# Reordering the start of a Fourier-mixing and ReGLU kernel: x first, weights later, the second batch's bounce sooner

## The chip, the cores and the metric

One core of one Trainium2 chip runs the whole kernel. The metric is the device time in microseconds (us) of one execution; a median over several runs is given. Runs more than 1.5% above a kernel's fastest would be left out. A "span" is the time from the first to the last instruction of the one execution that was profiled; it is some 2 us below the device time.

## The reference, cut to what matters

```python
def _attn_ref(x, filt_r, filt_i):              # x: 8 batches of 3008 x 256
    X = np.fft.rfft(x, axis=1)
    Y = X * (filt_r + 1j * filt_i)[None]
    return np.fft.irfft(Y, n=x.shape[1], axis=1)

def _moe_ref(x, w_gate, w_val, w_out):         # 24064 tokens, 256 -> 1536 -> 256
    return (np.maximum(x @ w_gate, 0) * (x @ w_val)) @ w_out
```

Everything is float32 at the interface; the kernel works in bf16 after the first matmul.

## The kernel before

The length 3008 is split into 94 x 32. For each batch, stage A (a 94-point transform, `psA`) writes to DRAM (`Abuf`) and is read back transposed (`at`): this is "the bounce". Stage B does the forward 32-point transform (`psX`), the product with the filters (`tt`, `uu`) and the inverse (`psD`), and writes to DRAM again (`Dbuf`), which is read as `dC`. Stage C (`psY`) gives the tokens, and then the FFN runs in 47 blocks of 512 tokens with 12 steps each. From the first block on, the next batch's A, B and C are slipped into the steps of the FFN ("forward 0 of batch 1 at step 16"). Batch 0 and part of batch 1 have no FFN to hide in: that is the prologue, which the change touches.

Two queues of transfers matter. The sync engine issues x, tables, `Abuf`, `at`, `Dbuf`, `dC`, strictly in program order, each waiting for its data. GpSimd issues filters and weights, which are cast from float32 to bf16 on the way. Both run on the same 16 DMA engines (the DMA views below give each queue's share of them).

```python
    load_x(0, nc.sync, ((0, 0, 2 * q), (0, 2 * q, 4 * q), (1, 0, 2 * q)))
    nc.sync.dma_start(F2, ...)                     # tables
    nc.sync.dma_start(tabs, ...)
    load_x(0, nc.sync, ((1, 2 * q, 4 * q),))
    ...
    hold_gpsimd(XF[0][:, 2 * q - 8:2 * q])         # GpSimd waits for the first half of tile 0
    load_filters()
    load_own_filters()
    warm(11)
    for i, f in enumerate(items_a(0)):             # 16 items of A, fillers between them
        f()
        if i >= 13: make_back_t(i - 13)
        else:       warm(1, 256)
        ...
    # bounce, copies of the filters to their places, more fillers
    hold_gpsimd(ats[0][0:32, NG - 1, 0:8])         # bounce is in
    load_vg(0, DFF // 2)                           # first half of the two input weights
    nc.sync.dma_start(gate, ats[0][0:32, NG - 1, 0:8])   # the sync queue waits too
    load_x(1, nc.sync, ...)
    first_b(amid)                                  # B of batch 0, with items of A of batch 1
    load_d(0, 0, 1)                                # first quarter of dC
    # a 1-row read of Dbuf makes GpSimd wait for D
    load_vg(DFF // 2, DFF)                         # second half
    load_o()                                       # output weights
    for f in early: f()                            # the rest of A of batch 1
    ... # [cut] in the steps of the FFN: load_d(0, 1..3) at 0, 9, 14;
        # load_at(1, 0..3) at 3; forwards of batch 1 at 16, 23, 26, 29, 35, 40
```

## Time and profile before

| | before |
|---|---|
| device time, median of the runs beside the changed kernel | 907.38 us |
| span of the profiled run | 905.5 us |
| TensorE busy, whole span | 97% |
| first matmul of A / last end of A | 7.46 / 23.77 us |
| first forward of B (bounce is in) / first product | 33.44 / 33.89 us |
| last inverse of B ends | 54.55 us |
| first `psY` of C | 62.83 us |
| forward 0 of batch 1 | 87.63 us, at step 16 |

A row of the timeline names what ran and when it started; these moments are simply the first or last row of a tile. The stretches, the chain and the waits themselves are shown in the prediction.

### The profile page before, as it was taken

What the parts mean: (1) busy time and instruction counts of PE and PEld (TensorE: products, weight loads), DVE (VectorE), ACT (ScalarE), POOL (GpSimd) and SP (SyncE); (2) the same over time, 40 slices, a digit from 0 to 9 for tenths busy, and PEclk for the clock granted to TensorE, in tenths of its full rate; (3) what the DMA queues carried; (4) which work ended last, traced back from release to release, by engine and by line L of the source; (5) the groups of instructions that cost most, each with busy time, mean ns of one, the idle gap of its engine ahead of it and who ended that gap; (6) DMA issues with size and microseconds to landing.
All of it is one profiled execution on the core that took longest, in us unless ns stands there. A gap on an engine that the chain in (4) does not pass through costs nothing.

```text
span 905.5 us, 19111 instructions
## 1 busy us (share of the span) xinstructions
PE 875.3 (97%) x7096; PEld 512.1 (57%) x7217; DVE 566.6 (63%) x872; ACT 498.6 (55%) x891; POOL 359.0 (40%) x351
## 2 busy tenths in 40 slices
PE   8797899999999999999999999999999999999997
PEld 3343565556555665566655566556655556666665
DVE  2635776567665776657766677657766577655553
ACT  4474556555555555555655565655565555555552
POOL 4342667117680386614763166811768000000000
PEclk9899999999999999999999999999999999999999
DMA  9979337623475344663364533754346512331111
GB/s 254 245 219 220 101 95 177 141 80 109 122 175 118 90 126 122 141 134 112 96 161 128 119 98 101 182 116 100 108 136 158 116 31 82 78 75 36 37 32 51
DMA packets 113662, 109.17 MB, mean 121 GB/s; under 512 B 20290, under 2 KB 98370, under 8 KB 112834
## 3 DMA queue, kind: packets, MB, share of 16 engines
q1 hardware_dynamic: 91078, 81.72, 35.3%
q0 software_dynamic: 22176, 26.01, 11.7%
q8 instruction: 57, 0.93, 0.5%
q10 hardware_dynamic: 316, 0.22, 0.1%
q14 instruction: 35, 0.29, 0.1%
HBM read 61.93 MB, written 49.81 MB: 123 GB/s over the span
## 4 chain that ended last, share of the span: by engine, by line
PE 86%; DVE 4%; DMA 4%; ACT 3%; issue 1%; SPq 1%; POOL 0%; DVEq 0%; POOLq 0%
PE psG L464 25%; PE psO L483 25%; PE psV L464 24%; DVE prod L469 4%; PE psA L276 3%; PE psF L322 3%; ACT vsb L467 3%; PE psD L393 2%; PE psX L363 2%; PE psY L448 1%; DMA XF<-in_x_dram 1%; DMA dC<-Dbuf 1%; DMA Abuf<-asb 1%; DMA out_dram<-osb 0%; DMA at<-Abuf 0%
## 5 line engine op out<-in xcount | busy, mean ns | idle before, releaser
L469 DVE SCALAR_TENSOR_TENSOR prod<-psG,vsb 128x512 bf16<-128x512 f32 x564 | 389.0, 690 | 271.3 <-ACT vsb L467 265.8
L467 ACT CAST vsb<-psV 128x512 bf16<-128x512 f32 x564 | 333.0, 590 | 266.8 <-PE psV L464 211.7
L483 PE MATMUL psO<-WoT,prod 128*128 128x256 bf16 x2256 | 336.6, 273 | 1.5
L464 PE MATMUL psG<-yT,WgT 128*128 128x512 bf16 x1099 | 329.1, 379 | 7.4 <-DMA WgT<-in_moe_w_gate_dram 2.5
L464 PE MATMUL psV<-yT,WvT 128*128 128x512 bf16 x1037 | 316.9, 380 | 0.7 <-ACT yT L453 0.4
L483 PEld LDWEIGHTS <-prod 128*128 128x128 bf16 x2256 | 220.7, 98 | 143.4
L464 PEld LDWEIGHTS <-WgT 128*128 128x128 bf16 x1128 | 109.9, 98 | 136.9 <-DMA WgT<-in_moe_w_gate_dram 3.0
L464 PEld LDWEIGHTS <-WvT 128*128 128x128 bf16 x1128 | 98.1, 98 | 41.8 <-issue 30.4
L258 POOL CAST scr<-yT 128x8 f32<-128x8 bf16 x24 | 4.6, 191 | 265.8 <-ACT yT L453 265.8
L379 DVE TENSOR_TENSOR tt<-psX,Ftr 128x512 bf16<-128x512 f32 x96 | 65.0, 682 | 12.9 <-PE psX L363 12.9
L400 ACT CAST dsb<-psD 128x512 bf16<-128x512 f32 x96 | 51.5, 589 | 28.5 <-PE psD L393 28.4
L308 POOL TENSOR_TENSOR fold<-XP 128x1024 f32<-128x1024 f32 x24 | 56.5, 2356 | 25.1 <-PE psF L322 24.9
L489 ACT COPY osb<-psO 128x512 f32<-128x512 f32 x92 | 54.5, 593 | 20.6 <-PE psO L483 20.3
L379 DVE TENSOR_TENSOR uu<-psX,Fti 128x512 bf16<-128x512 f32 x89 | 60.6, 681 | 0.0
L309 POOL TENSOR_TENSOR XP<-XP 128x1024 f32<-128x1024 f32 x24 | 56.4, 2350 | 1.9
L295 POOL DMA_DIRECT2D XP<-in_x_dram x96 | 56.4, 592 | 0.9 <-issue 0.5
L453 ACT CAST yT<-psY 128x512 bf16<-128x512 f32 x47 | 27.6, 586 | 26.2 <-PE psY L448 26.2
L329 DVE CAST asb<-psF 128x512 bf16<-128x512 f32 x48 | 30.9, 686 | 17.3 <-PE psF L322 12.9
L329 ACT CAST asb<-psF 128x512 bf16<-128x512 f32 x48 | 25.8, 589 | 27.3 <-PE psF L322 27.3
L448 PE MATMUL psY<-M,dC 96*128 96x94 bf16 (+18 forms) x604 | 37.7, 198 | 1.1 <-DMA dC<-Dbuf 1.1
L455 DVE CAST yT<-psY 128x512 bf16<-128x512 f32 x47 | 32.0, 681 | 9.8 <-PE psY L448 9.8
L448 PEld LDWEIGHTS <-dC 96*128 96x128 bf16 x604 | 34.5, 97 | 4.6 <-DMA dC<-Dbuf 1.2
(66 smaller groups left out, 481.6 us busy)
## 6 DMA issues: line engine op xcount, KB each, us to landing
at<-Abuf SPq DMA_DIRECT2D x32, 384.0 KB
dC<-Dbuf SPq DMA_DIRECT2D x64, 192.0 KB
XP<-in_x_dram POOLq DMA_DIRECT2D x48, 256.0 KB, 5.9
Dbuf<-dsb SPq DMA_DIRECT2D x23, 512.0 KB
XP<-in_x_dram POOLq DMA_DIRECT2D x96, 96.0 KB, 2.7
Abuf<-asb SPq DMA_DIRECT2D x96, 96.0 KB
out_dram<-osb SPq DMA_DIRECT2D x70, 94.0 KB
XF<-in_x_dram SPq DMA_DIRECT2D x18, 256.0 KB
```

Of the source, the lines that this page charges most:

```text
L295: nc.gpsimd.dma_start(xp[r:r + 24, 0:4:2, :], _ap(x, (b * N1 * N2 + o) * D, [[N2 * D, 24], [47 * N2 * D, 2], [1, 512]]))
L308: tt(t, xp[:, 0:2], xp[:, 2:4], op=ALU.add)
L309: tt(xp[:, 2:4], xp[:, 0:2], xp[:, 2:4], op=ALU.subtract)
L329: copy(asf[:, :, q, :], banks[q])
L379: nc.vector.tensor_tensor(p, psX, filt, op=ALU.mult)
L400: nc.scalar.copy(dsb[:, a, o:o + 2, :], psD[a])
L448: nc.tensor.matmul(psY[:, o:o + w], dCs[b, n2 // 8][:, n2 % 8, h * 128:(h + 1) * 128], M1[:, n1:n1 + w], start=True, stop=True)
L464: nc.tensor.matmul(pt[:, :W], w[:, h, ft * 128:(ft + 1) * 128], yt[:, h, :], start=(h == 0), stop=(h == 1))
L467: nc.scalar.copy(vsb, psV[:, :W])
L469: nc.vector.scalar_tensor_tensor(prod, in0=psG[:, :W], scalar=0.0, in1=vsb, op0=ALU.max, op1=ALU.mult)
L483: nc.tensor.matmul(psO[:, t % 2], prods[ft][:, t * 128:(t + 1) * 128], WoT[:, ft, :], start=(ft == 0), stop=(ft == NFT - 1))
L489: copy(osb[:, t0 % 2:t % 2 + 1], psO[:, t0 % 2:t % 2 + 1])
```

## The change

The intent, in the order of the prologue: get x in ahead of everything, run A without fillers, start x of batch 1 right behind the bounce without a gate, keep the weights off the engines until B is under way, and do the second batch's reads of `at` and its forwards sooner.

```diff
-    nc.vector.memset(XF[0][:, 0:q], 0.0)
-    nc.gpsimd.memset(XF[0][:, q:2 * q], 0.0)
+    nc.gpsimd.memset(XF[0][:, 0:q // 2], 0.0)
+    nc.vector.memset(XF[0][:, q // 2:q], 0.0)
...
-    load_x(0, nc.sync, ((0, 0, 2 * q), (0, 2 * q, 4 * q), (1, 0, 2 * q)))
+    load_x(0, nc.sync, ((0, 0, q), (0, q, 2 * q), (0, 2 * q, 4 * q), (1, 0, 2 * q), (1, 2 * q, 4 * q)))
     ... F2, tabs ...
-    load_x(0, nc.sync, ((1, 2 * q, 4 * q),))
-    hold_gpsimd(XF[0][:, 2 * q - 8:2 * q])
+    hold_gpsimd(XF[1][:, 2 * q - 8:2 * q])
...
-        if i >= 13:                      # inside A
-            make_back_t(i - 13)
-        else:
-            warm(1, 256)
+    for i in range(3):                   # behind A
+        make_back_t(i)
+        warm(6)
...
-    warm(18)
+    warm(6)
...
-    hold_gpsimd(ats[0][0:32, NG - 1, 0:8])
-    load_vg(0, DFF // 2)
-    nc.sync.dma_start(gate, ats[0][0:32, NG - 1, 0:8])
     load_x(1, nc.sync, ...)
...
-            for _ in range(2 if i > 2 else 1):          # items of A of batch 1 in B: 1, 2, 2, 2
+            for _ in range((1, 2, 2, 2, 1)[i - 2]):     # and one more between the last inverses
+        if i == 2:
+            load_vg(0, DFF // 2)
...
     load_d(0, 0, 1)
     ...
+    for c in range(2):
+        load_at(1, c)
...
-            for c in range(4):
-                at_step(3, lambda c=c: load_at(1, c))
+            for c in range(2, 4):
+                at_step(c - 2, lambda c=c: load_at(1, c))
...
-        for i, l in enumerate((-35, -28, -25, -22, -16, -11, -4) if b == 1 else
-                              (-40, -35, -28, -23, -16, -11, -4)):
+        for i, l in enumerate((-40, -35, -28, -23, -16, -11, -4)):
```

The last hunk puts the six forwards of batch 1 at steps 11, 16, 23, 28, 35 and 40.

More of the change, by code (lines that the diff above doesn't have):

```diff
@@ L154 @@
     Abuf = [dram.tile([NROW * N2, D], BF16, name=f"Abuf{b}") for b in range(B)]
-    gate = dram.tile([32, 8], BF16, name="gate")
     Dbuf = [dram.tile([NROW * N2, D], BF16, name=f"Dbuf{b}") for b in range(B)]
@@ L416, in first_b @@
         inv(0, 4, cuts=cuts)
+        amid(6)
         inv(0, 5, cuts=cuts)
@@ L511 @@
     q = NX2 * D // 4
-    nc.vector.memset(XF[0][:, 0:q], 0.0)
+    nc.gpsimd.memset(XF[0][:, 0:q // 2], 0.0)
+    nc.vector.memset(XF[0][:, q // 2:q], 0.0)
+    nc.vector.memset(junk, 1.0)
     nc.gpsimd.memset(XF[0][:, q:2 * q], 0.0)
-    nc.vector.memset(junk, 1.0)
     nc.vector.memset(XF[0][:, 2 * q:3 * q], 0.0)
```

## The prediction

> **What bounds the kernel now.** I read the busy table by stretch first, because the change touches only the start and a mean over 905 us hides it. Columns: stretch in us, its length, then busy time of TensorE, its weight loads, VectorE, ScalarE and GpSimd, granted clock, DMA share, GB/s.
>
> ```profile
> 0.00:33.40 33.40, 29.37 (x142) 11.37 (x143) 14.30 (x24) 15.11 (x21) 10.58 (x20) 1.00 0.92 254
> 33.40:54.50 21.10, 15.57 (x165) 6.81 (x165) 10.54 (x17) 12.27 (x23) 9.58 (x10) 0.84 0.81 240
> 54.50:63.90 9.40, 8.58 (x34) 3.38 (x31) 0.40 (x1) 7.32 (x14) 4.82 (x6) 1.00 0.71 186
> 63.90:112.00 48.10, 40.27 (x299) 22.08 (x305) 29.69 (x46) 23.36 (x42) 23.63 (x24) 1.00 0.77 170
> 112.00:905.50 793.50, 781.55 (x6463) 468.51 (x6574) 511.71 (x785) 440.54 (x793) 310.42 (x292) 1.00 0.43 108
> ```
>
> The stretches are: stage A of batch 0 and its bounce through DRAM; stage B (forward, product, inverse) with the first part of A of batch 1; the D writes with the rest of that A; the first blocks of the FFN; everything after. The last has TensorE busy 781.55 of 793.50 us, and the diff leaves its work alone. So the change can save only in the first 112 us: about 5.5 us of TensorE holes in B and 7.8 us in the first blocks, plus whatever A, the bounce and the clock give.
>
> Second, the chain of waits from 20 us on (start, length, what):
>
> ```profile
> 23.80 0.59 ACT asb L279
> ...
> 24.41 5.40 DMA Abuf<-asb
> ...
> 29.83 3.48 DMA at<-Abuf
> ...
> 33.40 0.31 SPq L555
> ...
> 34.98 6.99 DMA XF<-in_x_dram
> ...
> 42.11 1.99 PE psA L276 x2
> ```
>
> The bounce costs 9.5 us after the last eviction of A. Then x of batch 1, held back by the gate transfer, ends a wait in the middle of B. The waits of TensorE in B and then the busy table in two-microsecond stretches show what follows:
>
> ```profile
> PE psA L276 <- DMA XF<-in_x_dram: 3.8, 1, 3.8
> ```
>
> ```profile
> 42.00:44.00 2.00, 1.89 (x2) 0.39 (x2) 0.00 (x0) 0.00 (x0) 0.22 (x1) 0.50 1.08 337
> 44.00:46.00 2.00, 2.00 (x26) 1.30 (x26) 1.29 (x3) 1.02 (x2) 0.00 (x0) 0.50 1.17 425
> 46.00:48.00 2.00, 2.00 (x4) 0.45 (x2) 0.60 (x1) 1.80 (x4) 0.65 (x1) 0.72 0.98 411
> ```
>
> After 3.8 us of waiting TensorE runs at half clock to about 46.9 us. Last, the waits of TensorE from 63.9 to 112 us (total, times, longest):
>
> ```profile
> PE psG L464 <- DMA WgT<-in_moe_w_gate_dram: 2.5, 1, 2.5
> PE psX L363 <- DVE uu L379: 2.2, 2, 1.1
> PE psX L363 <- issue: 1.8, 1, 1.8
> PE psY L448 <- DMA dC<-Dbuf: 0.7, 1, 0.7
> ```
>
> The 1.8 us at 85.84 has no named releaser; the DMA share falls there, and I read it as the landing of `at` of batch 1.
>
> **What the skill says.** The Trainium skill, "TensorE: Matmul & The Clock Gate", Part 1: an idle window of about 3.4 us puts the array back to half clock. The trace agrees: 3.8 us of wait, then a clock of 0.50. "DMA: Bandwidth & Descriptors", section "Issuing engines are not separate DMA queues": transfers of all issuing engines run on the same 16 DMA engines and interleave. The trace agrees: from 12 to 24 us the software queue (filters) has 62.0% and the hardware queue 48.2% of them. This matters most: reordering the prologue removes no byte. Same page, "Anatomy of one DMA": about 2 us are fixed per DMA; filters first issued at 8.03 us begin to move after 10 us here.
>
> **Part by part.**
>
> 1. *Memsets and x in finer pieces.* The first x issue needed two memsets of 0.91 and 0.95 us and came at 2.02; now it needs two half as long and comes at about 1.6. The first piece is half the bytes. The first landing was 7.33; I expect about 6.3. The opening fillers end at 6.85 and move up with the memset of their operand by 0.5 us, so A starts at about 6.4 instead of 7.46.
>
> 2. *A without filler.* An item costs 0.86 (two fp32 matmuls) and a filler 0.11. Thirteen fillers (1.4 us) and three table transposes with their hand-overs (0.28 plus about 0.17 each, 1.3 us) leave A. 16 x 0.86 = 13.8 us, so A ends at about 20.3 plus half a microsecond of waiting for x, against 23.78. All x lands earlier: the hardware queue moved 0.73 MB from 8 to 10 us, 0.36 MB/us, when x had the engines alone; 3.08 MB from about 4 us on are then in by about 13, before A's thirteenth item asks for the last quarter.
>
> 3. *After A.* TensorE now does three transposes with six fillers (3 x 1.56), three second tables with six (3 x 1.49) and six more (1.28): 10.4 us, so it reaches B not before 20.8 + 10.4 = 31.2. Before, it got there at 32.56 and then waited 0.88 for the bounce.
>
> 4. *Filters.* They are held until the third quarter of x is in: 2.3 MB from 4 us at 0.36 MB/us and a microsecond to land, about 11.4 us instead of 7.49. By two-microsecond stretches of the queues, the filters used 477% of 2 us, 9.5 us of all 16 engines, and got some 75% of them once x was through. Starting to move 2.9 us after that, at 14.3, 9.5 / 0.75 = 12.7 us end at 27. Before it was about the same, since x starved them to 16 us; their small own-table rows landed at 28.1. From there VectorE has a fixed tail: one copy 0.95, three small ones 0.56, three copies 2.80, two of 0.2, together 4.7 us. That gives 32.8 for the first product (33.89 before). The bounce should end near 31.5: A's last write starts 3 us earlier, but the same filters and now x of batch 1 share the engines. B therefore starts in effect at about 32.5 instead of 33.44: a gain of only 0.9 out of the 3 us that A gives.
>
> 5. *B.* No gate, no first weights ahead: x of batch 1 is issued from about 27 and its first half is in by 35, and B asks for it at 37.4 (4.9 us in). The wait of 3.8 goes, and the half clock with it: 42.1 to 46.9 at half rate is 2.4 us. Added: one A item, 0.86, moved from behind B into it; ScalarE's 14.7 us of evictions and copies in B leave little slack, so I add 0.5. B goes from 21.0 to 21.0 - 3.8 - 2.4 + 0.9 + 0.5 = 16.2. It ends at 48.7 against 54.48: 5.8 earlier.
>
> 6. *D to the first block.* 8.35 us from B's last inverse to the first psY are two DMA latencies (Dbuf, dC); the moved item was hidden under them. Unchanged.
>
> 7. *First blocks.* Second weights still wait for D, so the 2.5 of WgT and 0.7 of dC stay. `at` of batch 1 is issued earlier, but forward 0 of batch 1 also moves from step 16 to 11, so its 1.8 us stay about as they are: from D on, the hardware queue must move 3.1 MB ahead of it at the 0.15 MB/us it had beside the weights, 20.5 us, or 24.8 after B's end; step 11 comes 22.4 after it. Spreading the six forwards over steps 11 to 40 instead of 16 to 40 thins VectorE's products: 2.2 us of waits for it and most of the 2.3 us of holes from 100 to 112 (the same 2.2 seen twice) go. I take 2.2, plus 0.3.
>
> Sum: 0.9 (start of B) + 4.8 (B) + 0 + 2.5 = 8.2 us; 907.2 - 8.2 = 899.0.
>
> **Rivals.** (a) *The DMA engines are the bound of the prologue.* Their share is 0.92 to 33.4 us, so filters that start 4 us later end 3 us later, the product starts at 36, and x of batch 1 in the same queue as the bounce makes it worse. For it: the share; against: about 1.8 us idle from 30 to 33, and x leaves room for filters after 14. Time then: about 902. (b) *B gives back nothing:* ScalarE or the third-engine products pace it at 18 us and more, or an idle at its start still drops the clock: about 901. (c) *All three gains compound:* B starts at 31.2, x and `at` are always there, the weight stall shrinks because less is left to write after D: 6 us of holes in the first blocks go, about 893. (d) *The new forward 0 waits 5 us for `at`* at step 11: about 902. I see nothing that reaches the 18 us of 2%: all of it together, 5.5 of holes in B, 2.4 of clock, 7.8 in the first blocks and 3 from A, is about 19 us, and most of it has a reason to stay.
>
> **Range and chances.** Parts 4, 5 and 7 each carry 2 us either way and are nearly independent, so 3.5 us in all (the root of three squares of 2), a little more for 8 in 10. Predicted 899.0, from 894.5 to 903.0; the repeat runs of before, 906.06 to 908.50, add little. Faster by over 2% 0.02, within 2% 0.975, slower 0.005.
>
> **What would show it.** Right: A's last matmul at about 20.8; the wait of psA on XF in B gone, clock 1.00 there; B's last inverse near 48.7; WgT wait still near 2.5; no VectorE wait of psX from 90 to 112; the stretch from step 60 on as long as before. Wrong: first product after 34 with VectorE waiting on Ftr or Fti (rival a), a clock below 1 in B (b), a WgT wait under 1 us (c), psX waiting over 4 us at step 11 (d).

## The result, and the profile after

The changed kernel took 908.53 us (median of four, 907.55 to 908.82) against 907.38 us for the kernel before in the same rounds. Ratios in this document are the mean time of one kernel's fast runs over the mean of the other's fast runs of the same rounds, so not quite the ratio of the medians: here 1.0011, with a 95% interval of 0.9994 to 1.0029. The two are the same to within noise; the predicted gain of 8.2 us did not appear, and the measured time lies above the predicted 894.5 to 903.0 us.

The busy table of the changed kernel over the same stretches as in the prediction, with the same columns:

```profile
0.00:33.40 33.40, 28.69 (x134) 11.34 (x136) 10.60 (x19) 15.09 (x21) 11.64 (x21) 1.00 0.90 243
33.40:54.50 21.10, 17.04 (x170) 7.22 (x171) 13.82 (x23) 14.44 (x28) 9.45 (x9) 0.92 0.84 251
54.50:63.90 9.40, 6.54 (x26) 2.78 (x25) 0.00 (x0) 4.59 (x9) 4.52 (x6) 0.95 0.78 220
63.90:112.00 48.10, 40.86 (x297) 22.19 (x300) 29.07 (x45) 22.54 (x41) 22.04 (x23) 0.90 0.73 162
112.00:905.50 793.50, 782.48 (x6469) 469.08 (x6581) 512.25 (x786) 441.11 (x795) 311.65 (x294) 1.00 0.43 108
```

(The stretches are cut where the stages of the kernel before ended; the changed kernel's B runs from 35.86 to 53.14.) B has fewer holes than before (17.04 us busy of 21.10, against 15.57) and a higher clock (0.92 against 0.84), as intended. But the clock in the first FFN blocks has fallen from 1.00 to 0.90, and the stretch ahead of them has more idle time. The waits of TensorE up to 112 us in the changed kernel (total us, times, longest) name the places:

```profile
PE psY L448 <- DMA dC<-Dbuf: 9.3, 2, 6.4
PE psX L362 <- DMA at<-Abuf: 3.5, 1, 3.5
...
PE psA L275 <- DMA XF<-in_x_dram: 1.5, 1, 1.5
```

The wait for x in B (3.8 us) and the wait for the gate weights (2.5 us) are gone. In their place stand 3.5 us for the bounce of batch 0, 2.9 us for the first quarter of `dC` and 6.4 us for the second. The waits for VectorE, 2.2 us before, are gone too.

Moments of each kernel's profiled run, in us from its start (first or last row of the tile in the timeline):

| | end of A | first forward of B | first product | end of B | first `psY` | forward 0 of batch 1 | first `psO` |
|---|---|---|---|---|---|---|---|
| before | 23.77 | 33.44 | 33.89 | 54.55 | 62.83 | 87.63 (step 16) | 80.04 |
| predicted | 20.8 | | 32.8 | 48.7 | 57.1 | | |
| after | 21.45 | 35.86 | 36.80 | 53.14 | 63.04 | 84.64 (step 11) | 86.27 |

(57.1 is the predicted end of B plus the 8.35 us that the prediction gave to D.) These moments, and those below, are of one profiled execution each. The runs whose program is the changed kernel's up to the point in question put the first forward at 35.5 to 36.2 us, the end of B at 53.1 to 54.3 and, for the changed kernel and e10, the first `psY` at 63.04 and 61.90: a difference of under about 1 us between two kernels says little. A really ends 2.3 us sooner. Then the kernel loses 4.7 us between the end of A and the first forward, wins back 3.8 us in B, loses 1.6 us behind it, and another 6 us up to the first `psO`, the start of block 1 (forward 0, 0.8 us, is now ahead of it). From there to the end it wins most of that back.

The first loss is seen in the sync queue's own timeline. Rows give the start of the issues, the time from first to last, and how many. The kernel before:

```profile
24.41 0.31 SPq L281 DMA_DIRECT2D Abuf<-asb  x1
24.82 5.59 SPq L349 DMA_DIRECT2D at<-Abuf  x3
33.40 0.31 SPq L555 DMA_DIRECT2D gate<-at  x1
```

And the changed one:

```profile
22.09 0.31 SPq L280 DMA_DIRECT2D Abuf<-asb  x1
22.50 9.95 SPq L348 DMA_DIRECT2D at<-Abuf  x3
32.50 5.74 SPq L176 DMA_DIRECT2D XF<-in_x_dram  x9
```

The last of the three `at` issues waits for the last `Abuf` write. That write took 5.4 us before (24.41 to 29.81, in the chain that the prediction shows) and 9.8 us after (22.09 to the last `at` issue at 31.87). It was issued 2.3 us earlier and landed 2 us later. Who was on the engines meanwhile is told by the DMA view of the changed kernel for 16 to 32 us (queue, packets, MB, share of the 16 engines); q0 is GpSimd's queue:

```profile
q0 software_dynamic: 1824, 1.54, 61.8%
```

All 1824 packets of the filters fall into these 16 us: they took 61.8% of all engines just while A's output was being written. The filters themselves were late too. VectorE's timeline of the changed kernel (start, length, what, and in brackets how long it had waited for what):

```profile
32.07 0.95 DVE L237 COPY Ftr<-Ftr 32x3072 bf16<-32x3072 bf16 x1 [3.28 <-DMA Ftr<-in_filt_r_dram]
```

In the kernel before this copy started at 28.21, after a wait of 0.5 us. The rest of VectorE's copies follow it without a gap and end at 36.77, and the first product starts at 36.80, 0.94 us behind the first forward. So two things held up the start of B in the changed kernel, the bounce and the filters, and an edit that mends one of them meets the other.

### The profile page after: what moved, and what is told of

The parts are those of the page before. It is cut to its first block, busy times and chain, and to the rows that moved or that the text cites. A ratio compares the mean times of both kernels' runs of the same rounds, so it can differ in the third digit from the quotient of the medians.

```text
span 906.6 us, 19099 instructions
## 1 busy us (share of the span) xinstructions
PE 875.6 (97%) x7088; PEld 512.6 (57%) x7210; DVE 565.7 (62%) x872; ACT 497.8 (55%) x891; POOL 359.3 (40%) x351
## 3 DMA queue, kind: packets, MB, share of 16 engines
q0 software_dynamic: 22176, 26.01, 11.8%
## 4 chain that ended last, share of the span: by engine, by line
PE 85%; DVE 4%; ACT 4%; DMA 3%; issue 1%; SPq 1%; POOL 0%; ACTq 0%
PE psG L464 25%; PE psO L483 25%; PE psV L464 24%; DVE prod L469 4%; ACT vsb L467 3%; PE psF L321 3%; PE psD L392 2%; PE psA L275 2%; DMA dC<-Dbuf 2%; PE psX L362 2%; PE psY L448 1%; PE psJ L508 1%; DMA out_dram<-osb 1%; DMA Dbuf<-dsb 1%; SPq L176 1%
## 5 line engine op out<-in xcount | busy, mean ns | idle before, releaser
L489 ACT COPY osb<-psO 128x512 f32<-128x512 f32 x92 | 54.6, 593 | 20.1 <-PE psO L483 19.5
L328 DVE CAST asb<-psF 128x512 bf16<-128x512 f32 x48 | 30.9, 686 | 17.3 <-PE psF L321 13.8
```

The lines of the kernel that those rows point to most:

```text
L328: copy(asf[:, :, q, :], banks[q])
L489: copy(osb[:, t0 % 2:t % 2 + 1], psO[:, t0 % 2:t % 2 + 1])
```

## The experiments

Two theories were set up after this. **Theory 1**: the 16 DMA engines carry a fixed load until the first forward of batch 1, and are full for nearly all of it; reordering decides only which consumer waits. Its second part, **1a**, is about the first FFN blocks: what sets them is the bounce of batch 1 beside the second half of the weights, whichever wait is named. **The rivals**: single misplaced transfers, each costing its own wait and nothing else: the filters' late release, x of batch 1 behind the bounce (theory 2 below), the weights amid B, the order of `dC` and `at`. Twelve kernels were run, each with five timed rounds beside the kernel before. All are edits of the changed kernel unless said otherwise.

| run | median us | ratio to before (95%) | first forward of B | end of B | first `psY` | forward 0 of batch 1 |
|---|---|---|---|---|---|---|
| changed kernel | 908.53 | 1.0011 (0.9994 to 1.0029) | 35.86 | 53.14 | 63.04 | 84.64 |
| e1 filters early | 907.78 | 1.0018 (1.0000 to 1.0037) | 35.67 | 52.44 | 62.10 | 84.17 |
| e2 gate for x | 908.81 | 1.0026 (1.0011 to 1.0042) | 36.41 | 55.15 | 63.91 | 85.14 |
| e3 weights ahead of B | 907.18 | 1.0010 (0.9994 to 1.0026) | 35.72 | 53.64 | 61.58 | 82.89 |
| e4 `dC` first | 915.03 | 1.0099 (1.0079 to 1.0119) | 35.62 | 54.32 | 62.82 | 88.78 |
| e5 spread alone, on before | 912.16 | 1.0056 (1.0028 to 1.0085) | 33.42 | 53.59 | 61.88 | 86.66 |
| e6 second half amid B | 904.03 | 0.9965 (0.9936 to 0.9993) | 36.15 | 53.10 | 62.95 | 79.44 |
| e7 all weights amid B | 905.15 | 0.9978 (0.9949 to 1.0007) | 35.62 | 53.30 | 66.23 | 79.53 |
| e8 no filters (wrong result) | 905.79 | 0.9988 (0.9956 to 1.0020) | 32.60 | 50.67 | 60.25 | 81.97 |
| e9 coarse x | 908.13 | 1.0021 (1.0007 to 1.0034) | 34.33 | 53.69 | 61.69 | 84.58 |
| e10 old steps | 912.22 | 1.0063 (1.0050 to 1.0075) | 35.54 | 53.28 | 61.90 | 89.82 (step 16) |
| e11 e6 with the old prologue | 900.94 | 0.9947 (0.9934 to 0.9959) | 34.13 | 51.78 | 61.81 | 76.61 |
| e12 e6, filters early, coarse x | 901.23 | 0.9946 (0.9933 to 0.9958) | 33.94 | 50.91 | 61.52 | 77.14 |

e1 to e4 shared a chip and its runs of before, so did e5 to e8, and e9 to e12. The median of before was 906.27, 905.89 and 906.13 us there, so across groups the ratios are compared, not the medians. Two of the eleven runs of before in the group of e5 to e8 took 911.93 and 912.44 us, the other nine 904.58 to 907.87; none is over the 1.5%, so all are kept, but without the two the mean of before would be 1.15 us lower, and the ratios of e5 to e8 0.0013 higher.

### e1: the filters released as before

```diff
-    hold_gpsimd(XF[1][:, 2 * q - 8:2 * q])
+    hold_gpsimd(XF[0][:, 2 * q - 8:2 * q])
```

> The changed kernel with the filters released as before the change, by the first half of x instead of the third quarter. Theory 1 (the 16 DMA engines carry a fixed load in the prologue; whoever is put first delays the rest): the filters are first issued near 8 us instead of 14.35, the last filter copy starts near 28 instead of 32.07 and the first product near 33.3 instead of 36.80, while x lands later and stage A ends near 23 instead of 21.45; at of batch 0 lands near 33.5 instead of 35.86; total 905.5 to 907. Theory 2 (x of batch 1 right behind the bounce is what delays the bounce): nothing at the start of B moves by more than 1 us, total 908.5.

The filters came early: VectorE made its four copies of `Ftr` from 27.77 us on without waiting for a transfer. The last of them started at 30.7, not near 28, because A and the tables ahead of the copies were later. A slowed as expected, ending at 23.31. But the bounce was no earlier: the first forward stayed at 35.67, and the first product stood at 36.11, not near 33.3. By the letter this is theory 2's forecast (nothing at the start of B moves by more than 1 us); it is e2 that rules theory 2 out. The last write of `Abuf` was issued later, at 25.27, landed at about 31.9 as in the changed kernel, and with it the reads. The early filters took engine time from x and from the writes, and what VectorE gained the bounce did not. In total there is no gain.

### e2: the gate put back

```diff
     place_nyq()
+    nc.sync.dma_start(gate, ats[0][0:32, NG - 1, 0:8])
     load_x(1, nc.sync, ...)
```

> The changed kernel with the gate transfer put back ahead of x of batch 1. Theory 1: x of batch 1 was issued only from 32.50 us, so it cannot have delayed much: at of batch 0 lands within 0.7 us of 35.86, and the wait of psA for XF in B is back with 2 to 4 us and a half clock; total 910 to 913. Theory 2: at lands 2 us or more earlier, near 33.5, and the total stays at 907 to 909.

The first forward came at 36.41, within 0.6 us of the changed kernel: x of batch 1 did not delay the bounce, and theory 2 falls. The second half of the expectation missed. B lasts 18.7 us instead of 17.3 (but e4, whose B is the changed kernel's, lasted as long), and only about half a microsecond of recorded waiting for x came back, not 2 to 4, and the total, 908.81, is below the expected 910 to 913. So the gate alone did not cause the 3.8 us wait of the kernel before. There the first weights ran beside x as well. e3 and e11 below have these weights beside x and no gate, and no wait either: it took both.

### e3: the first half of the weights ahead of B

```diff
     place_nyq()
+    hold_gpsimd(ats[0][0:32, NG - 1, 0:8])
+    load_vg(0, DFF // 2)
     load_x(1, nc.sync, ...)
...
-        if i == 2:
-            load_vg(0, DFF // 2)
```

> The changed kernel with the first half of the weights issued ahead of B again instead of behind the fifth GpSimd product. Theory 1: the last write of Dbuf takes about 2.5 us from issue to landing instead of 4.78, but x of batch 1 now shares the engines with the weights and psA waits 1 to 3 us for it in B; B ends up to 3 us later, the first psY within 1.5 us of 63.04; total 907 to 910. Rival (the weights amid B are the one thing that spoils the change): no new wait in B, first psY near 60.5, total near 905.5.

The last write of D is where an effect was looked for. A row of the chain of waits, first of the changed kernel, then of e3, then of e4, which has the weights amid B (start, length, what):

```profile
54.31 4.78 DMA Dbuf<-dsb
```

```profile
54.82 3.13 DMA Dbuf<-dsb
```

```profile
55.49 3.14 DMA Dbuf<-dsb
```

Without the weights amid B, D's last write took 1.65 us less, and first `psY` comes 1.5 us earlier although B ends half a microsecond later. But e4 shows that the weights need not cost this. The cost goes with how long before D's write they were issued: 9.4 us in the changed kernel, e1 and e8, where the write took 4.7 to 4.8 us; 10.2 to 10.6 in e10, e2 and e4, where it took 3.8, 3.7 and 3.1; 12.0 in e9, where it took 3.1. The expected wait for x in B did not appear, against theory 1. That the total is nevertheless unchanged (1.0010 against 1.0011, either to within 0.0017) fits theory 1: the second quarter of `dC` was still waited for, 6.4 us as in the changed kernel. Forward 0 came 1.75 us sooner, which these intervals cannot resolve.

### e4: the second quarter of `dC` first

```diff
-    load_d(0, 0, 1)
+    load_d(0, 0, 2)
...
-    for s, z in ((0, 1), (9, 2), (14, 3)):
+    for s, z in ((9, 2), (14, 3)):
```

> The changed kernel with the second quarter of dC issued right behind the first, ahead of at of batch 1 and of the last two Abuf writes. Theory 1: the wait of psY for dC of 6.4 us shrinks under 1, but the forward at step 11 now waits 2 to 5 us for at, or WgT waits again; total 903.5 to 906.5. Rival (one misplaced transfer, nothing behind it): the 6.4 us and the half clock after it (1.9 us) go without a new wait, total 900 to 901.

This is the run that decides between one misplaced transfer and theory 1a. The waits of TensorE in e4, to set beside those of the changed kernel above:

```profile
PE psX L362 <- DMA at<-Abuf: 15.8, 2, 12.5
...
PE psY L448 <- DMA dC<-Dbuf: 1.5, 1, 1.5
PE psG L464 <- DMA WgT<-in_moe_w_gate_dram: 1.0, 1, 1.0
```

The 6.4 us for `dC` are gone, and a wait of 12.5 us for `at` stands in their place, far more than the 2 to 5 us expected. The kernel became 8 us slower. Its chain of waits shows why (start, length, what):

```profile
70.26 11.29 DMA Abuf<-asb
81.56 7.13 DMA at<-Abuf
```

The last chunk of `Abuf` of batch 1 takes 11.3 us to be written, and only then can the last read of `at` start. It took as long (11.0) in the changed kernel. What e4 moved is its issue, from 65.94 to 70.26 us, since the sync queue keeps its order, and forward 0 came later by the same 4 us. So the wait for `dC` was only what showed; behind it stood the bounce of batch 1. In the changed kernel the last read of `at` was issued at 76.94; without the 6.43 us for `dC`, step 11 would have been reached near 78.2 (an estimate, 84.64 - 6.43), before that read, which took 4.4 us even in e11, could have landed.

### e5: only the spread of the forwards, on the kernel before

```diff
-        for i, l in enumerate((-35, -28, -25, -22, -16, -11, -4) if b == 1 else
-                              (-40, -35, -28, -23, -16, -11, -4)):
+        for i, l in enumerate((-40, -35, -28, -23, -16, -11, -4)):
```

> The kernel before with nothing but the forwards of batch 1 spread over steps 11 to 40 as after the change. Theory 1a (the chain that sets the first blocks is batch 1's own bounce: its last Abuf writes and the reads of at, which land at 84 to 88 us whatever the order, beside the second weights): forward 0 at step 11, reached near 76 us, waits 8 to 11 us for at instead of 1.8 at step 16, and the 2.2 us of waits for VectorE go; total 909 to 913. Rival (the spread is a plain gain of 2 to 4 us that the rest of the change gives away): a wait for at under 3 us, total 902 to 904.5.

```profile
PE psX L363 <- DMA at<-Abuf: 8.8, 2, 8.1
...
PE psG L464 <- DMA WgT<-in_moe_w_gate_dram: 2.3, 1, 2.3
```

As theory 1a expected: 8.1 us of waiting at step 11 in place of 1.8 at step 16, no waits for VectorE, and a loss of 0.56%. Asking five steps earlier does not bring the data earlier: forward 0 ran at 86.66 us, 1 us before the kernel before had it.

### e6 and e7: the later weights moved into B's gap

e6: the first half as in e3, the second half behind forward 2 in B, the output weights still behind D. e7: the output weights there too.

```diff
+    hold_gpsimd(ats[0][0:32, NG - 1, 0:8])
+    load_vg(0, DFF // 2)
     load_x(1, nc.sync, ...)
...
         if i == 2:
-            load_vg(0, DFF // 2)
+            load_vg(DFF // 2, DFF)
+            load_o()                      # e7 only
...
-    load_vg(DFF // 2, DFF)
-    load_o()                              # e7 only
```

> The changed kernel with the first half of the weights ahead of B (as in e3) and the second half amid B, so that only the output weights are loaded behind D. Theory 1a: the last write of Dbuf is as slow as after the change (4 to 5 us), first psY near 62.5, but at of batch 1 lands near 79 instead of 84 and dC near 73; forward 0 at step 11 runs near 80; total 902 to 905. Rival (order only, no gap to fill): same moment of forward 0, 84 to 85, total 907 to 909.

> As e6, with the output weights amid B too, so that no weights move behind D. Theory 1a: the engines are idle for some 4 us between 44 and 60, so the weights cost D up to 5 us (first psY 63 to 66), but at lands within 14 us of the last Abuf write, forward 0 near 77 to 79 without a wait over 2 us; total 899 to 903. Rival (the bytes merely move from one wait to another): first psY near 68 and total 906 to 909.

Both bear out what theory 1a expects of forward 0: with less to move behind D, forward 0 of batch 1 runs at 79.4 to 79.5 us instead of 84.64, though B ends at the same time. e6 is faster than before with an interval clear of 1 (0.9965, up to 0.9993). e7 pays on the other side: D is delayed, first `psY` comes at 66.23 us, 3.3 us later than in e6, and the total is not clear of the kernel before; 905.15 misses the expected 899 to 903.

### e8: no filters at all (a wrong result)

```diff
-    load_filters()
+    for _, dst in FILT:
+        nc.vector.memset(dst, 0.0)
```

> The changed kernel without the eight large filter transfers (the filters are cleared instead, so the result is wrong on purpose). Theory 1 (the engines are full up to the start of B): at of batch 0 lands before the fillers end near 32.3 instead of 35.86, the first product starts before 33.2 instead of 36.80, B ends 3.5 to 4 us earlier (49.5), and A ends as before at 21.5. Rival (latencies of the bounce, not the load, set the start of B): at lands within 1 us of 35.86, first product near 36.

The sync queue's timeline of this run:

```profile
22.44 0.31 SPq L280 DMA_DIRECT2D Abuf<-asb  x1
22.85 3.75 SPq L348 DMA_DIRECT2D at<-Abuf  x3
```

The last `at` issue came at 26.02, so the last `Abuf` write took 3.6 us instead of 9.8. TensorE waited for no bounce at all, and forward 0 of B ran behind the fillers at 32.60. That is shown, then: it was the filters on the same engines, not the latency of the bounce, that held up the first forward. The first product came at 34.34, later than expected, because the copies of the filters into place still ran behind the second tables on VectorE; B ended at 50.67 instead of 49.5. And the total fell by a quarter of a percent at most (ratios 0.9988 and 1.0011, whose intervals overlap). What was won at B's end was not lost again: B ended 2.5 us sooner, forward 0 ran 2.7 us sooner and the span was 2.0 us shorter. But no more than that came of 9.9 us less engine time: `dC` was still waited for, 5.3 us. This goes against theory 1 in its strong form. Up to forward 0 the engines moved 20.4 MB in the changed kernel and were busy for 93.8% of the time; here they moved 18.8 MB at 85.7%. The freed time was left unused, so what set forward 0 was not all the bytes ahead of it.

### e9: x in coarser pieces

```diff
-    load_x(0, nc.sync, ((0, 0, q), (0, q, 2 * q), (0, 2 * q, 4 * q), (1, 0, 2 * q), (1, 2 * q, 4 * q)))
+    load_x(0, nc.sync, ((0, 0, 2 * q), (0, 2 * q, 4 * q), (1, 0, 2 * q), (1, 2 * q, 4 * q)))
```

> The changed kernel with the first half of the first x tile loaded in one piece of 256 KB a transfer again instead of two of 128 KB (12 transfers for x instead of 15). Theory 1: the sync queue issues a transfer every 0.63 us whatever its size, so small first pieces left the engines at 40 to 85% until 10 us; with fewer, x ends 1 to 2 us sooner, the filters follow by as much, and the bounce of batch 0 lands near 34.7 instead of 35.86 although A starts later (7.2 instead of 5.82); total 907 to 908. Rival (early start of A is what counts): A ends 1.3 us later and at lands 1 us later, total 909.5.

The sync queue's share of the engines from 4 to 10 us (packets, MB, share), of the kernel before, of the changed one and of e9:

```profile
q1 hardware_dynamic: 345, 1.91, 91.4%
```

```profile
q1 hardware_dynamic: 366, 1.45, 78.0%
```

```profile
q1 hardware_dynamic: 307, 1.68, 82.6%
```

The finer pieces of the change left 0.46 MB unmoved in these 6 us; coarse pieces get half of that back. (The 0.63 us per issue hold for x; an issue of `Abuf` took 0.31.) A starts at 7.68 instead of 5.82 and yet ends at the same time, 21.62, and the first forward comes 1.5 us sooner. The early start of A was worth nothing. The total did not follow here either: the second wait for `dC` grew to 7.6 us and forward 0 of batch 1 stayed at 84.58.

### e10: the forwards at their old steps

The tuple of the kernel before in the changed kernel (the reverse of e5).

> The changed kernel with the forwards of batch 1 at their old steps (16, 23, 26, 29, 35, 40). Theory 1a: the wait for dC of 6.4 us stays, at is in before step 16 so no wait for it, and the waits of psX for VectorE near 100 us (2.2 us and about as much again) are back: total 909 to 911, so the spread was worth 1 to 3 us here, where at came in time, and cost 6 in e5, where it did not. Rival (the spread has no worth): total within 0.7 of the changed kernel, 908 to 909.

The stretch from 100 to 112 us, with the columns of the busy table, in the kernel before, in e10 and in the changed kernel:

```profile
100.00:112.00 12.00, 9.72 (x93) 5.70 (x94) 8.74 (x14) 5.82 (x12) 8.39 (x6) 1.00 0.36 111
```

```profile
100.00:112.00 12.00, 10.04 (x98) 5.76 (x95) 8.92 (x15) 6.63 (x12) 10.86 (x8) 1.00 0.41 125
```

```profile
100.00:112.00 12.00, 11.89 (x117) 7.33 (x118) 8.39 (x14) 6.88 (x13) 11.66 (x11) 1.00 0.51 145
```

Three forwards within six steps (23, 26, 29) crowd VectorE, and TensorE has two microseconds of holes; spread out, it has 0.1. With the old steps the changed kernel is 0.6% slower than the kernel before (1.0063), 0.5% slower than with the new ones. The loss is larger than the 1 to 3 us expected and than the profiled run shows: that run, at 909.76, was the fastest of e10's five, and where the others lost 2 to 3 us more is not seen.

### e11 and e12: two combinations

e11 is e6 with the kernel before's whole prologue up to the filter copies (order of x and tables, early filters, fillers inside A), still without the gate. e12 is e6 with only the edits of e1 and e9.

> e6 with the whole prologue of the kernel before (order of x, tables and filters, fillers in A), but without the gate. Theory 1: the old order gets the bounce through by 33.5 to 34.5, x of batch 1 is in time for B without the gate (wait under 1 us), B ends at 50.5 to 52, forward 0 of batch 1 at 77 to 78; total 900.5 to 902.5, faster than e6 and than before. Rival (the bytes only wait elsewhere): forward 0 at 79 to 80 as in e6, total 903 to 904.5.

> e6 with the filters released as early as before and x in coarse pieces, the rest of the new prologue kept. Theory 1: between e6 and e11: at of batch 0 near 35, forward 0 near 78.5, total 901.5 to 903.5. Rival: no different from e6, 904.

Both came out as expected or a little better (forward 0 of both and e12's total lie just below the expected ranges) and beat both kernels, by half a percent of the kernel before (0.9947 and 0.9946, both intervals below 0.996). The waits of TensorE in e11:

```profile
PE psY L448 <- DMA dC<-Dbuf: 3.7, 2, 3.0
...
PE psD L392 <- POOL uu L376: 1.4, 2, 0.8
PE psX L362 <- DMA at<-Abuf: 1.2, 1, 1.2
```

and its chain of waits between D and forward 0 of batch 1:

```profile
60.67 11.40 DMA Abuf<-asb
72.15 4.42 DMA at<-Abuf
```

It is still the bounce of batch 1 that sets forward 0, at 76.61 us; it is only sooner. It is not faster in the part that theory 1a named, though: the `Abuf` write takes 11.4 us here, with only the output weights beside it. Taking the runs together shows where the time was saved:

| us | end of B to issue of the last `Abuf` write | to issue of the last read of `at` | to forward 0 |
|---|---|---|---|
| changed kernel | 12.8 | 11.0 | 7.7 |
| e4 `dC` first | 15.9 | 11.3 | 7.2 |
| e6 second half amid B | 9.0 | 11.3 | 6.0 |
| e7 all weights amid B | 11.8 | 6.4 | 8.1 |
| e8 no filters | 13.5 | 10.9 | 6.9 |
| e11 | 8.9 | 11.5 | 4.5 |

(The last column is the read's landing at most; of these runs only e4's forward 0 waited for it by the list of waits.) The write is shorter only where no weights at all move behind D (e7). Most of what e6 and e11 won is the first column: the write is issued sooner. The two last issues of `Abuf` in the sync queue's timeline, in the changed kernel and in e6:

```profile
61.41 5.05 SPq L280 DMA_DIRECT2D Abuf<-asb  x2
```

```profile
61.45 1.29 SPq L280 DMA_DIRECT2D Abuf<-asb  x2
```

The first of the two alone took 4.49 us in the changed kernel and 0.64 in e6, and the second quarter of `dC` stands behind it in the queue. All runs of the new order with the second half of the weights behind D have such a stall, of 3.6 to 5.3 us; e6, e7, e11 and e12 have none (0.63 or 0.64). So the weights act on the queue that must issue the bounce, and not only on its transfers. Why an issue is held up is not shown.

One more sum holds across the runs: from forward 0 at step 11 to the end of its span the changed kernel takes 822.0 us (906.6 - 84.64), and the eleven other kernels that have it at step 11 take 821.7 to 823.8. The total follows the moment of forward 0. The two prologues are equally good once the weights are out of the way, so the new A without fillers has no value of its own.

## Why the prediction was wrong, point by point

The size of the result (within 2%) was rightly called near certain, and every wait that the prediction said would go did go. The sum failed: 8.2 us of gain were predicted and the span grew by 1.1, so 9.3 us are missing. They are in four terms. Of the other signs of being wrong that it had written down, a clock below 1 in B (0.92) and a WgT wait under 1 us (none) came true too, the latter without the gain that rival (c) expected; no wait of over 4 us for `at` showed at step 11.

- **Parts 1 and 2, A**: the mechanism was right and A's end nearly so (21.45 against 20.8). "All x lands earlier" was wrong. The prediction took the rate of the engines and forgot the rate of issue, which the timeline of the kernel before already showed: nine issues in 5.69 us, 0.63 us each. After the change it is fifteen in 9.51. The third quarter of x released the filters at 13.80, not at 11.4.
- **Part 4, the start of B, failed by 3.4 us** (35.86 against 32.5). It reckoned 12.7 us for the filters, from 14.3 to 27, and they took from 16 to about 31.5. The step "the bounce should end near 31.5" named the competition and then did not charge for it: the last `Abuf` write took 9.8 us. e8 shows that the filters were the cause, and e2 that x of batch 1 was not. This is rival (a), which the prediction set at 902 and let go; the sign it had written down for it, a first product after 34 with VectorE waiting for `Ftr`, came true (36.80, and a wait of 3.3 us). Only its clause on x of batch 1 did not, by e2.
- **Part 5, B, failed by 1.1 us** (17.3 against 16.2). The 3.8 us wait and its half clock went, but the new 3.55 us wait ahead of B brought a half clock of its own: 0.50 between 36 and 38 us in the changed kernel. That the lost clock is the whole of the 1.1 us was not tested, and 1.1 us is within what B's length varied by between runs of the same B (17.3 and 18.7 in the changed kernel and e4).
- **Part 6, "unchanged", failed by 1.5 us** (9.9 against 8.35). The first weights, moved amid B, were still on the engines when D was written: its last write took 4.78 us, and 3.13 in e3 without them. In e4 and e9, where the same weights had a microsecond or more longer to pass, it took 3.1 as well.
- **Part 7, the first blocks, failed by 3.4 us**: a gain of 2.5 was predicted, and from first `psY` to the end of the span the changed kernel took 0.9 us longer (843.6 against 842.7). The spread's gain was real (e10: 0.5% by the timed runs, though only 1.4 us in the profiled one, so whether it is more than the 2.2 reckoned stays open). But "the 2.5 of WgT and 0.7 of dC stay" was wrong: the first went, and the second became 6.4, with a clock of 0.50 to 0.64 up to 84 us behind it. Its estimate that `at` would be in 24.8 us behind B was too low: in the kernel before and in e5, where TensorE waited for it, it came 33.1 us behind B (87.63 less 54.55, 86.66 less 53.59). In the changed kernel the wait for `dC` covered this; e4 uncovers it. The step that failed is that the sync queue would move 3.1 MB at a steady 0.15 MB/us: its issues stalled for 4.5 us behind D, and one write and one read then took 11.0 and up to 7.7 us in a row.

All four have one omission in common. The prediction quoted the rule that all queues share 16 engines, saw a share of 0.92, and then reckoned each transfer's delay by itself. The change left the engines under-used at the start (fine pieces) and in two gaps (the two queues together had 0.1% of them from 44 to 46 us and 9.0% from 58 to 60), kept the second half of the weights behind D, beside the bounce of batch 1, and put the first request for that bounce five steps earlier. That bounce and the second quarter of `dC` set forward 0, and forward 0 set the total. Savings ahead of B's end did reach it as far as B's end moved (e8: 2.5 us, then 2.7), but e1 and e9 moved B's end by less than a microsecond. Moving the second half of the weights brought forward 0 sooner by 5 us (e6) to 8 us (e11, with the old prologue), with nearly the same bytes ahead of it (20.1 and 19.9 MB, the engines 96.6% and 98.2% busy).

What stays open: why an issue of the sync queue is held up for 4.5 us beside the second half of the weights, why e10's other runs were slower than its profiled one, and how much of e11's last 3.0 us for `dC` could still go.

## What to carry to other kernels

When the transfers of a prologue fill the DMA engines, a reordering can move waits without removing any; look for the consumer whose moment the total follows (here forward 0 of batch 1, with some 822 us behind it in every run that has it at step 11), and judge every edit by the moment at which that consumer runs. A gain there comes from filling the engines' idle stretches with loads that would otherwise fall into the full one (e6), not from giving the earliest stage a better start. In a queue that issues in order, look at when a transfer was issued as well as at how long it took: the bounce's write took 11 us in e4, e6 and e11 alike. And a wait that is named last may only hide the next one: taking away `dC`'s 6.4 us brought out 12.5 us for `at`, some 4 of them because e4 had also put the bounce later in its queue.

## What the Trainium skill lacked or had wrong

- "DMA: Bandwidth & Descriptors", section "Issuing engines are not separate DMA queues", says that the sequencer's time to initiate a DMA is usually small relative to the DMA itself. Here the sync queue issued x at one DMA every 0.63 us, of 256 KB or of 128 KB alike, and 1.45 MB moved from 4 to 10 us with its first six pieces of 128 KB, instead of 1.91 (1.68 in e9, with none). One issue of `Abuf` took 4.49 us in the changed kernel and 0.64 in e6; the page has no figure for an issue that is held up.
- The same page, section "Anatomy of one DMA", gives a fixed 2.0 us plus the bytes over 436 GB/s for a DMA issued by GpSimd, which for 384 KB would be an estimate of 2.9 us. The write of 384 KB issued on the sync queue took 3.6 us without the filters, 5.4 in the kernel before and 9.8 in the changed one. The page says that queues interleave, but has no figure for what a DMA of one queue takes beside a busy second one.
- "TensorE: Matmul & The Clock Gate", Part 1, puts the return to half clock after an idle window of about 3.4 us. In the changed kernel a gap of 2.86 us ahead of first `psY` was enough: the clock was 0.74 from 62 to 64 us and 0.50 from 64 to 66. In e1 one of 2.63 us was (0.68, then 0.50), and in the kernel before one of 2.54 us, ending at 72.64, was not (1.00). (Ends of matmuls are modelled in the trace, so the gap is known only to within a matmul or so.)
